# Both query tiles of two steps cast together and transposed together by DMA, a step ahead of their use

## The chip, the cores and the metric

The kernel runs on one core of one Trainium2 chip. In this kernel TensorE runs the matmuls; ScalarE, VectorE and GpSimd run the casts, copies and elementwise work; SyncE issues the DMA transfers. A transfer has landed when all of its data have arrived. The span is the time from the first to the last instruction of one profiled execution, and the granted clock is TensorE's clock as a share of full speed. The metric is the device time of one execution in microseconds, lower is better. An execution counts as slow when it lies over 1.5% above the fastest of the same kernel. A ratio here is the mean time of one kernel's fast runs over the mean of the other's fast runs of the same rounds, so it is not quite the ratio of the medians that I quote.

## The reference

A recurrent retention layer (decay per head) feeds a multiplicative feed-forward layer without a nonlinearity. Cut to what matters:

```python
# q, k, v: (4 batches, 8 heads, 768 positions, 64), fp32
for t in range(S):
    state = gamma * state + outer(k[:, :, t], v[:, :, t])
    y[:, :, t] = (1 / sqrt(D)) * q[:, :, t] @ state
x = y.transpose(0, 2, 1, 3).reshape(3072, 512)
out = ((x @ w1) * (x @ w2)) @ w3 @ w_out        # (3072, 512), fp32
```

## The kernel before

The recurrence is cut into chunks of 128 positions, two batches at a time: 12 steps. Step m begins on TensorE with the state part of the step before (`inter(m - 1)`), then the scores of chunk m, then the output matmuls of the feed-forward of two steps ago, then the feed-forward of the step before, with intra (the outputs from within the chunk) and kv (the update of the state) between. The scores need the queries and keys with the head dimension on the partitions, so q and k are cast to fp16 and then transposed by a DMA.

One query tile holds one batch and two chunks. So tiles 6 and 7 are read by steps 6 and 7, tiles 8 and 9 by steps 8 and 9, and the first half of the scores of a step (16 matmuls) reads the even tile, the second half the odd one.

```python
def load_q(n):                      # 512 KB, SyncE queue
    g, e = divmod(n, 2)
    ...
    dma_in(t[...], q[bp * 2 + e, :, cp * 2 * C : (cp + 1) * 2 * C, :]...)

def q_cast(n, eng):                 # fp32 -> fp16, two buffers
    q16 = att.tile([128, 1024], HP, tag="q16", name="q16", bufs=2)
    (nc.scalar.copy if eng is nc.scalar else eng.tensor_copy)(q16[...], q_in.pop(n)[...])

def q_dma(n):                       # transpose, five buffers, SyncE queue
    qT = att.tile([128, 2, NP, 128], HP, tag="qT", name="qT", bufs=5)
    nc.sync.dma_start_transpose(qT[...], q16s.pop(n)[:, :])

def queries(m, e, p, s, r):
    ...
    return qTs[m // 2 * 2 + e][half(r), :, p, i0 : i0 + 32]
```

Every load, every DMA transpose and every output of the kernel is issued by SyncE, in the order of the program. This is the step, which sets that order:

```python
def step(m):
    inter(m - 1); outputs_back(m - 1, 0); outputs_back(m - 1, 1)
    ...
    am_back = scores(m)
    am_back(0); am_back(1)
    if m > 5:
        q_dma(m + 2)
    ffn[m - 2].o_unit(0)            # 8 output matmuls, copy on ScalarE, output DMA
    if m + 1 < NSTEP:
        k_cast(m + 1, (nc.scalar,))
        k_dma(m + 1)                # transpose of k for the next step
    ffn[m - 2].o_unit(1)
    load_k(m + 2)
    load_v(m + 2)
    load_q(m + 3 if m < 6 else m + 4)
    for f in range(2):
        ffn[m - 1].ab(f)
    if m == 5:
        q_cast(7, nc.scalar)
        q_dma(7)
        load_q(9)
    intra(m)
    ...                             # kv, more ab
    v_cast(m + 1, (nc.gpsimd, nc.gpsimd))
    if m == 4:
        q_cast(6, nc.gpsimd)
        q_dma(6)
    elif m > 4:
        q_cast(m + 3, nc.gpsimd)
    ...
```

## Time and profile before

| | before |
|---|---|
| median of three runs | 198.76 us (197.88 to 199.11) |
| span of the profiled run | 196.1 us |
| TensorE busy | 92% |
| granted clock, mean | 0.983 |
| scores of step 4 start at | 73.70 us |
| step 6, from its scores to those of step 7 | 19.85 us |
| steps 4, 5, 7, 8, 9, 10, likewise | 12.16 to 12.24 us |

The prediction below shows the page, the stretches and the chain of waits. Two more views belong beside them. First the timeline of SyncE around step 5; columns: start, length, engine and line, operation, target and source, count. L60 is a load, L313 the transpose of q, L335 that of k, L490 an output. A line in which several are merged includes the waits between them.

```profile
87.57 2.48 SPq L313 DMA_TRANSPOSE qT<-q  x1
...
92.82 1.23 SPq L60 DMA_DIRECT2D stg<-in_k_dram  x2
94.09 3.05 SPq L60 DMA_DIRECT2D stg<-in_v_dram  x2
97.19 1.02 SPq L60 DMA_DIRECT2D stg<-in_q_dram  x1
98.31 2.36 SPq L313 DMA_TRANSPOSE qT<-q  x1
```

The first line is tile 6, the last tile 7. What to look for is the time SyncE spends on issuing: the two v loads alone take 3.05 us of its time. The timeline of TensorE has the other end of it; in brackets the idle time before the line and what ended it:

```profile
98.13 0.29 PE L358 MATMUL psA<-qT,kT 64*64 64x64 f16 x12
103.59 0.43 PE L358 MATMUL psA<-qT,kT 64*64 64x64 f16 x16 [5.16 <-DMA qT<-q]
```

The first half of the scores of step 6, on tile 6, runs at 98.13, and the second half waits 5.16 us for tile 7.

### The profile page before, as it was taken

How to read it: one execution, taken by the hardware profiler on the slowest of the kernel's cores; microseconds unless marked ns; L12 is line 12 of the kernel's file. 1: busy time of each engine (PE TensorE's matmuls, PEld its weight loads, DVE VectorE, ACT ScalarE, POOL GpSimd, SP SyncE). 2: the span in 40 equal slices, each digit the busy share in tenths (PEclk: the TensorE clock that was granted, in tenths of full speed). 3: DMA queues.
4: the chain of work that ended last, by engine and by line, in shares of the span. 5: the costliest groups of instructions: out<-in, count | busy, mean ns of one | idle time of the engine just before them, and what ended most of it. 6: DMA issues, size and time to landing. Idle time of an engine off the chain costs nothing.

```text
span 196.1 us, 6231 instructions
## 1 busy us (share of the span) xinstructions
PE 180.8 (92%) x2651; PEld 126.8 (65%) x2651; DVE 96.7 (49%) x187; ACT 87.5 (45%) x165; POOL 64.1 (33%) x92
## 2 busy tenths in 40 slices
PE   7799998679998999999908999999999999999993
PEld 2355655558675785877803685877858678586772
DVE  1226356068378255674432265664556735555240
ACT  5578545475553544327400544325443264232432
POOL 6200233536618071280601044280732607120000
PEclk9999999999999999999995899999999999999999
DMA  6999999999999999999998696989969550110202
GB/s 213 370 390 384 255 278 344 270 357 250 231 220 238 253 205 234 226 244 215 258 229 154 166 233 162 243 206 187 207 162 215 116 160 3 57 53 3 107 0 107
DMA packets 87338, 40.23 MB, mean 205 GB/s; under 512 B 67728, under 2 KB 82320, under 8 KB 87312
## 3 DMA queue, kind: packets, MB, share of 16 engines
q1 hardware_dynamic: 87312, 39.85, 84.0%
q8 instruction: 20, 0.33, 0.7%
q14 instruction: 6, 0.05, 0.1%
HBM read 29.36 MB, written 6.29 MB: 182 GB/s over the span
## 4 chain that ended last, share of the span: by engine, by line
PE 68%; SPq 12%; DMA 11%; DVE 4%; ACT 1%; issue 1%; DVEq 0%; ACTq 0%
PE psF L460 33%; PE psO L485 23%; SPq L60 12%; DMA stg<-in_moe_w_out_dram 4%; DMA stg<-in_k_dram 4%; DMA qT<-q 3%; PE psY L431 3%; PE psA L358 2%; PE psG L460 2%; PE psY L380 2%; PE psF L570 1%; DVE ht L475 1%; PE psK L400 1%; DVE am L365 1%; PE psTk L330 1%
## 5 line engine op out<-in xcount | busy, mean ns | idle before, releaser
L460 PE MATMUL psF<-xt,w 128*128 128x256 f16 x672 | 77.1, 273 | 0.0
L460 PEld LDWEIGHTS <-w 128*128 128x128 f16 x704 | 68.0, 98 | 10.3
L475 DVE TENSOR_TENSOR ht<-pa,psF 128x256 f16<-128x256 f32 x88 | 36.6, 420 | 54.3 <-ACT pa L469 29.7
L418 POOL TENSOR_TENSOR t<-s,GS 128x512 f16<-128x512 f32 x19 | 24.1, 1267 | 71.8 <-DVE s L417 71.8
L469 ACT COPY pa<-psF 128x256 f32<-128x256 f32 x80 | 29.7, 371 | 39.9 <-PE psF L460 39.9
L485 PE MATMUL psO<-w3o,ht 128*128 128x512 f16 (+2 forms) x200 | 46.2, 386 | 0.0
L485 PEld LDWEIGHTS <-ht 128*128 128x128 f16 x200 | 19.2, 101 | 21.5 <-issue 3.3
L489 ACT ACTIVATE osb<-psO 128x512 f32<-128x512 f32 (+2 forms) x25 | 14.5, 580 | 40.0 <-PE psO L485 40.0
L290 POOL TENSOR_TENSOR v<-stg,VS 128x512 f16<-128x512 f32 x23 | 23.5, 1042 | 5.5 <-DMA stg<-in_v_dram 3.9
L365 DVE TENSOR_TENSOR am<-psA,keep 128x512 f16<-128x512 f32 x24 | 15.3, 679 | 7.0 <-PE psA L358 7.0
L440 DVE TENSOR_TENSOR xt<-psY,YS 128x512 f16<-128x512 f32 x24 | 16.1, 722 | 1.7 <-PE psY L431 0.8
L269 POOL CAST q<-stg 128x1024 f16<-128x1024 f32 x8 | 8.3, 1036 | 23.6 <-DMA stg<-in_q_dram 23.6
L417 DVE TENSOR_TENSOR s<-psK,t 128x512 f32<-128x512 f32 x20 | 13.8, 688 | 3.4 <-PE psK L400 2.7
L283 ACT CAST k<-stg 128x1024 f16<-128x1024 f32 (+1 forms) x12 | 11.2, 934 | 5.1 <-DMA stg<-in_k_dram 4.9
L358 PE MATMUL psA<-qT,kT 64*64 64x64 f16 x384 | 6.6, 197 | 6.6 <-DMA qT<-q 5.2
L215 DVE COPY w3t<-psW 128x1024 f16<-128x1024 f16 x8 | 5.4, 689 | 11.7 <-PE psW L223 9.2
L358 PEld LDWEIGHTS <-kT 64*64 64x64 f16 x384 | 5.1, 108 | 8.1 <-issue 5.9
L196 ACT CAST w3h<-stg 128x1024 f16<-128x1024 f32 x8 | 8.3, 1043 | 3.6 <-DMA stg<-in_moe_w_dram 3.5
L431 PEld LDWEIGHTS <-t 64*64 64x64 f16 x352 | 6.5, 109 | 3.6 <-issue 2.1
L503 PE MATMUL psZ<-zeros 128*128 128x512 f16 x19 | 7.6, 553 | 1.3 <-DVE zeros L142 1.3
L431 PE MATMUL psY<-qT,t 64*64 64x64 f16 x352 | 7.8, 194 | 0.7 <-DVE t L418 0.6
L244 PE MATMUL psW<-wo,w3t 128*128 128x512 f16 x32 | 8.4, 399 | 0.0
(58 smaller groups left out, 121.2 us busy)
## 6 DMA issues: line engine op xcount, KB each, us to landing
stg<-in_moe_w_dram SPq DMA_DIRECT2D x16, 512.0 KB, 6.6
stg<-in_q_dram SPq DMA_DIRECT2D x12, 512.0 KB, 6.9
stg<-in_k_dram SPq DMA_DIRECT2D x24, 256.0 KB, 5.4
stg<-in_v_dram SPq DMA_DIRECT2D x24, 256.0 KB, 5.2
out_dram<-osb SPq DMA_DIRECT2D x23, 256.0 KB, 2.5
stg<-in_moe_w_out_dram SPq DMA_DIRECT2D x4, 512.0 KB, 7.8
out_dram<-osb SPq DMA_DIRECT2D x1, 160.0 KB, 1.8
qT<-q SPq DMA_TRANSPOSE x8, 4.0
```

Of the source, the lines that this page charges most:

```text
L60: nc.sync.dma_start(dst, src)
L290: eng.tensor_tensor(v16[:, e, :].rearrange("j (h d) -> j h d", d=D), v32[:, e, :].rearrange("j (h d) -> j h d", d=D), VS[:, :].unsqueeze(2 ...
L358: nc.tensor.matmul(ps[r][half(s), p * 2 + e, :], lhsT=kT[half(r), e, p, half(s)], rhs=queries(m, e, p, s, r), start=True, stop=True,)
L365: nc.vector.tensor_tensor(am[:, r, :, :], ps[r][:, :, :], keep[:, :].unsqueeze(1).broadcast_to((128, NP * 2, L)), MULT,)
L418: eng.tensor_tensor(t16[:, :], s32[:, :], gs, MULT)
L431: nc.tensor.matmul(ps[s][half(r), u, :], lhsT=t[s][half(r), u * L : (u + 1) * L], rhs=queries(m, e, p, s, r), start=False, stop=(e == 1 an ...
L440: nc.vector.tensor_tensor(XT[m][:, :, s, :].rearrange("p u (i t) -> p u t i", t=2), psYs[m][s][:, :, :].rearrange(order, t=2), YS[:, :, :] ...
L460: nc.tensor.matmul(ps[:, :], lhsT=W[d][:, f * 128 : (f + 1) * 128], rhs=self.x(d), start=(d == 0), stop=(d == 3),)
L469: nc.scalar.copy(self.pa[f][:, :], ps[:, :])
L475: nc.vector.tensor_tensor(self.HT[:, f, :], self.pa.pop(f)[:, :], ps[:, :], MULT)
L485: nc.tensor.matmul(psO[:, :], lhsT=self.HT[:, f, e * 128 : (e + 1) * 128], rhs=W3O[f][:, cs], start=(f == 0), stop=(f == 7),)
L489: nc.scalar.activation(osb[:, cs], psO[:, :], AF.Copy, scale=final_scale)
```

## The change

The intent is to have both tiles of a pair cast at the end of the even step and transposed at the front of the queue of the odd step, a whole step before the first matmul reads them. The special cases of steps 4 and 5 go. In even steps the query load moves ahead of the loads of k and v, so that it is there for the cast at the end of the same step. The whole diff:

```diff
--- before.py
+++ after.py
@@ -651,22 +651,20 @@
         am_back = scores(m)
         am_back(0)
         am_back(1)
-        if m > 5:
+        if m > 3 and m % 2:
+            q_dma(m + 1)
             q_dma(m + 2)
         ffn[m - 2].o_unit(0)
         if m + 1 < NSTEP:
             k_cast(m + 1, (nc.scalar,))
             k_dma(m + 1)
         ffn[m - 2].o_unit(1)
+        load_q(m + 3) if m % 2 == 0 else None
         load_k(m + 2)
         load_v(m + 2)
-        load_q(m + 3 if m < 6 else m + 4)
+        load_q(m + 3) if m % 2 else None
         for f in range(2):
             ffn[m - 1].ab(f)
-        if m == 5:
-            q_cast(7, nc.scalar)
-            q_dma(7)
-            load_q(9)
         intra(m)
         kv_back = kv(m)
         kv_back(0)
@@ -675,10 +673,8 @@
         kv_back(1)
         if m + 1 < NSTEP:
             v_cast(m + 1, (nc.gpsimd, nc.gpsimd))
-        if m == 4:
-            q_cast(6, nc.gpsimd)
-            q_dma(6)
-        elif m > 4:
+        if m % 2 == 0:
+            q_cast(m + 2, nc.gpsimd)
             q_cast(m + 3, nc.gpsimd)
         for f in range(4, 8):
             ffn[m - 1].ab(f)
```

## The prediction

> **What bounds the kernel now.** I read the page from the top: shares of the engines, then the span in 40 slices of 4.9 us (196.1 / 40), in tenths.
>
> ```profile
> span 196.1 us, 6231 instructions
> ...
> PE 180.8 (92%) x2651; PEld 126.8 (65%) x2651; DVE 96.7 (49%) x187; ACT 87.5 (45%) x165; POOL 64.1 (33%) x92
> ...
> PE   7799998679998999999908999999999999999993
> ...
> PEclk9999999999999999999995899999999999999999
> ```
>
> TensorE is busy for 92%; no other engine reaches 50%. From slice 10 on it stands at 8 or 9 (the last slice aside), except in slice 21 (98.0 to 102.9 us), where the digit is 0; right behind that hole the clock row dips to 5 and 8. So the kernel is bound by TensorE with one hole in it. I then cut the span where each step starts (at the inter matmuls of the step before). Stretches view, steps 4 to 8; columns: length, busy time of PE, PEld, DVE, ACT, POOL with counts, granted clock, DMA share, GB/s.
>
> ```profile
> 73.33:85.51 12.18, 12.18 (x213) 9.11 (x214) 7.08 (x14) 5.06 (x11) 4.53 (x5) 1.00 1.23 234
> 85.51:97.61 12.10, 12.10 (x194) 9.03 (x193) 6.57 (x13) 5.90 (x12) 5.30 (x6) 1.00 1.22 233
> 97.61:117.78 20.17, 15.01 (x213) 9.98 (x214) 7.18 (x14) 5.04 (x12) 3.25 (x3) 0.83 0.96 197
> 117.78:129.69 11.91, 11.91 (x196) 8.85 (x198) 6.99 (x14) 4.99 (x11) 5.52 (x6) 1.00 0.83 194
> 129.69:141.93 12.24, 12.24 (x213) 9.17 (x214) 6.99 (x14) 4.99 (x11) 5.51 (x6) 1.00 0.96 211
> ```
>
> Four steps last 11.9 to 12.2 us with TensorE always busy; step 6 lasts 20.17, with 5.16 us of it idle and a granted clock of 0.83. The mean of its four neighbours is 12.11, so step 6 costs 8.06 us too much. The chain of waits around it (start, length, what) says on what it stood:
>
> ```profile
> 94.09 2.04 SPq L60
> 96.13 0.04 issue
> 96.18 0.96 SPq L60
> 97.14 0.04 issue
> 97.19 1.02 SPq L60
> 98.21 0.05 issue
> 98.26 0.02 SPq L313
> 98.28 0.03 issue
> 98.31 5.24 DMA qT<-q
> 103.54 0.04 issue
> 103.59 0.43 PE psA L358 x12
> 104.02 6.03 PE psO L485 x16
> ```
>
> The scores of step 6 (L358) wait for a transposed query tile. Steps 6 and 7 read tiles 6 and 7; tile 6 was transposed at 87.57, so this is tile 7. SyncE issues its transpose only at 98.31, when the scores already want it, and it lands 5.24 us later. Yet its cast on ScalarE was finished at 93.15 (92.11 + 1.04, from the timeline of ScalarE). Between lie, in SyncE's order, one output, two k loads, two v loads and the load of tile 8: 92.16 to 98.21. Those 5.2 us in the queue are about the whole wait. Behind it, the 16 output matmuls take 6.03 us instead of the 3.56 us that the same 16 take in every step from 3 to 10.
>
> **What the Trainium skill says.** "TensorE: Matmul & The Clock Gate", Part 1, says that after an idle window of about 3.4 us the array falls to half clock and comes back after about as long a busy one. The trace agrees: 5.16 us idle, then 16 matmuls at 6.03 instead of 3.56, and a clock of 0.58 from 103.6 to 110.0. "DMA: Bandwidth & Descriptors", Anatomy of one DMA, says that the DMA engines do not wait on semaphores; the wait sits on the issuing sequencer. So what stands behind a waiting or slow issue in SyncE's program waits too: the 92.16 to 98.31 above. The same page, Rules for kernel authors, says to issue early and wait late, which is this change's intent. "GPSIMD Engine Reference", 4.1 Engine selection, calls one-input work there roughly line-rate; here the cast of a query tile takes 1036 ns on GpSimd and 1045 ns on ScalarE, so moving it costs nothing in itself.
>
> **The change part by part.** Steps 0 to 3 issue the same things in the same order, so up to about 81 us nothing moves. No matmul is added or removed.
>
> *Loads.* In even steps the query load goes ahead of k and v. Tile 7's load moves from 85.19 to about 81.1, where the k load stood. It landed 6.9 us after issue before (85.19 to the cast at 92.11), so now it lands at about 88. The k and v loads of that step go back by its issue of about 1.1 us; k lands some 5 us after issue, at about 88, and its cast started at 88.77: just in time. Tile 9's load leaves step 5, which so has one 512 KB load less.
>
> *Casts.* Both on GpSimd at the end of the even step, after the v casts (which ended at 86.5): tile 6 at 86.5 to 87.55 as before, tile 7 at 87.6 or 88 (when it has landed) to 89.1 at the latest. ScalarE loses 1.04 us in step 5. GpSimd then has nothing to do until 93.2 (the next state update, L418), so two casts fit; neither engine is on the path.
>
> *Transposes.* They become the first things in SyncE's queue in step 5: tile 6 at 87.57 as before, since it waited for the same cast, and tile 7 right after, between 89.1 and 90.1. An issue took 1.24 to 2.48 us and a landing 3.0 to 5.4 us. Tile 7 therefore lands at about 94 to 95.5, against 103.5 before and a need at 98.1. The wait is gone with 2.5 us to spare.
>
> *What goes behind.* The output and the transpose of k for step 6 were issued at 90.15 and 90.78; a further transpose ahead of them (1.24 to 2.48) puts k's at about 92 to 93.3, and with 3.8 to 5.7 us to landing (the extremes of steps 4 and 5) at 95.8 to 99. It is needed at 98.1. This is the one place with little room. The loads behind it have a whole step in hand.
>
> *Buffers.* Five transposed tiles are kept; tile 9 takes the place of tile 4, last read at the start of step 6, and it is transposed in step 7; tile 7's place was tile 2's, done with in step 4. Two cast tiles are kept and both are read before the next pair is cast. No new wait.
>
> *The sum.* Idle before the scores 5.16, plus half clock on the output matmuls 6.03 - 3.56 = 2.47: 7.63 us. By steps it is 8.06 (the scores and first blocks after the hole were slow too). I take 7.8. All of it is on the path, since TensorE is full on either side and nothing waits in its place. 198.76 - 7.8 = 191.0. Against it stands k's transpose in step 6: a chance of about 1 in 4 of a wait of about 1 us, 0.3 us on average. Prediction 191.3 us.
>
> **The rivals.** *A wait on k's transpose takes the place of the one on q.* For it: three transposes behind one another when the DMA share is 1.22. In step 2 to 3 the trace has just that: two query transposes at 64.84 and 66.5 and k's at 68.73, which landed 4.1 us later, with no wait on it. Against it: step 5 has a load less. If it happens, 0.3 to 1.5 us idle, too short for the clock to fall: 191.5 to 192.5. If it passed 3.4 us, the clock would fall too and most of the gain would be lost: 195 to 198; I give that 3%.
>
> *The DMA queues become the bound.* Without the hole the transfers no longer have 8 us to catch up. A step moves k, v, q and the output, 0.524 MB each, and two transposes of 0.262: 2.6 MB in 12.1 us, 217 GB/s. Steps 4 and 5 moved 234 and 233 GB/s with TensorE full. Odd steps now have three transposes, 2.9 MB or 238 GB/s, even ones 2.4 MB. So it fits on average, and loads are used one step or more later. A wait of up to 2 us in steps 7 or 9 would give 191.5 to 193.5; 10%.
>
> *The casts come late:* tile 9 is loaded in step 6 and cast at its end. The load stands 7.7 us into the step (81.1 - 73.4) and lands some 7 us later, 14.7 into it; the cast is wanted 14 us in. Its transpose then starts in step 7 perhaps 1 us late, in front of the outputs and k's transpose, which had over 4 us in hand in steps 7 and 8 (121.82 plus 3.1 against scores at 130.3). It is hidden.
>
> *The hole was a matter of one run:* the three timings of before lie within 197.88 to 199.11, so the hole of 7.8 us was in all.
>
> **Range and chances.** The best is 198.76 - 8.06 with the spread of the runs (0.9 below the median): 189.9. The worst that I give weight is a new wait of 2 to 3 us: 194. Within 2% means above 194.8, so over 3 us of new waits; with the two rivals that could do it I get 0.06, and 0.01 for slower by 2%.
>
> **What would show it.** Right: TensorE's row has no 0 and the clock no 5 after slice 10; step 6 lasts about 12.2 us; no wait of a matmul on a transposed query; ScalarE has three query casts in place of four and GpSimd nine; both transposes of a pair stand together ahead of the outputs in steps 5, 7 and 9. Wrong: a wait of L358 on the transpose of k in step 6 (first rival), waits on v or k casts in steps 7 to 9 (second), or a transpose of tile 9 that starts late in step 7 and takes the outputs with it (third).

## The result and the profile after

The changed kernel took 192.64 us (median of four runs: 192.71, 195.71, 192.57, 192.49; the second was a slow one), against 198.94 for the kernel before in the same rounds: ratio of the fast runs 0.9698, 95% interval 0.9648 to 0.9749. In three later batches it was 0.9571, 0.9629 and 0.9604, each with its own profile.

The page of the kernel after, parts 1 and 2:

```profile
span 191.0 us, 6232 instructions
...
PE   7799998768998969999999999999999999999993
...
PEclk9999999999999999999999999999999999999999
```

There is no 0 in the row of TensorE after the start and no dip in the clock. After slice 10 one lesser digit stands in slice 15 (a 6); it is explained below. The stretches view of the kernel after, cut 0.2 us after the scores of steps 6 and 7 begin (columns as in the prediction):

```profile
100.77:112.70 11.93, 11.93 (x216) 8.83 (x207) 6.85 (x14) 5.00 (x11) 2.50 (x3) 1.00 1.23 245
112.70:125.22 12.52, 12.32 (x231) 9.07 (x220) 6.85 (x15) 4.91 (x11) 6.77 (x7) 1.00 1.16 200
```

Step 6 now takes 11.93 us with TensorE busy in all of it; step 7 has 0.20 us of idle. The timeline of SyncE in steps 4 and 5 shows why:

```profile
83.43 0.42 SPq L60 DMA_DIRECT2D stg<-in_q_dram  x1
83.94 2.53 SPq L60 DMA_DIRECT2D stg<-in_k_dram  x2
86.57 2.55 SPq L60 DMA_DIRECT2D stg<-in_v_dram  x2
90.10 4.20 SPq L313 DMA_TRANSPOSE qT<-q  x2
94.39 0.54 SPq L490 DMA_DIRECT2D out_dram<-osb  x1
95.04 2.59 SPq L335 DMA_TRANSPOSE kT<-k  x1
```

Both transposes of q stand ahead of the outputs. The second was issued at 93.05 and landed 3.2 us later, at 96.25; the scores of step 6 began at 100.58. The transpose of k behind them landed 4.5 us after its issue, at 99.54: 1.0 us before the scores.

Where the time went, step by step, from the start of one step's scores to those of the next (us; the column at the right is the second profile of the changed kernel, from the first batch of experiments):

| stretch | before | after | after, second profile |
|---|---|---|---|
| start to scores of step 4 | 73.70 | 76.23 | 74.03 |
| step 4 | 12.18 | 12.18 | 12.18 |
| step 5 | 12.16 | 12.16 | 12.16 |
| step 6 | 19.85 | 11.93 | 11.93 |
| step 7 | 12.17 | 12.53 | 12.23 |
| steps 8 to 10 | 36.61 | 36.55 | 36.55 |
| scores of step 11 to end | 29.42 | 29.42 | 29.42 |
| span | 196.09 | 191.00 | 188.51 |

The change gave 7.92 us in step 6 in both profiles. In the first, 2.53 us of it are missing because the part before step 4 was longer, and 0.36 in step 7. Of the 2.53, 1.49 us are one wait in step 3; this is the timeline of TensorE there:

```profile
69.24 0.60 PE L460 MATMUL psF<-xt,w 128*128 128x256 f16 x4 [1.49 <-ACT osb L489]
```

On ScalarE an output copy stood behind the cast of k tile 4, which waited for its load. The same happened in small in step 7, where the timeline of ScalarE reads:

```profile
116.49 1.05 ACT L283 CAST k<-stg 128x1024 f16<-128x1024 f32 x1 [1.01 <-DMA stg<-in_k_dram]
117.44 0.59 ACT L489 ACTIVATE osb<-psO 128x512 f32<-128x512 f32 x1
```

The k load of an even step now stands behind the query load, and the cast of that k tile, one step later, waits; the output copy behind it frees a bank of PSUM (the memory that matmuls write to) late, and TensorE stops for 0.2 us. That the place of the k load is the reason is read from the traces and was not tested alone: in the four profiles of the changed kernel the k casts of steps 6, 8 and 10, whose loads stand ahead of a query load, never wait, and those of step 7 wait 0.52 to 1.01 us. The place is not the only reason: the k cast of step 4, whose load also stands ahead of a query load, waits 0.30 to 0.89 us.

### The profile page after: what moved, and what is told of

Its sections match the earlier page's. It is cut to its first block, busy times and chain, and to the rows that moved or that the text cites. A ratio compares the mean times of both kernels' runs of the same rounds, so it can differ in the third digit from the quotient of the medians.

```text
span 191.0 us, 6232 instructions
## 1 busy us (share of the span) xinstructions
PE 178.9 (94%) x2651; PEld 125.4 (66%) x2651; DVE 96.8 (51%) x187; ACT 86.0 (45%) x164; POOL 65.1 (34%) x93
## 4 chain that ended last, share of the span: by engine, by line
PE 65%; DMA 18%; SPq 10%; ACT 3%; issue 1%; DVE 0%; ACTq 0%
PE psF L460 37%; PE psO L485 20%; SPq L60 10%; DMA stg<-in_moe_w_dram 7%; DMA stg<-in_k_dram 7%; DMA stg<-in_moe_w_out_dram 5%; PE psY L431 3%; PE psY L380 2%; PE psA L358 2%; PE psK L400 1%; ACT w L196 1%; ACT k L283 1%; ACT osb L489 1%; PE psTk L330 0%; ACT kT L196 0%
## 5 line engine op out<-in xcount | busy, mean ns | idle before, releaser
L460 PE MATMUL psF<-xt,w 128*128 128x256 f16 x672 | 77.4, 273 | 1.7 <-ACT osb L489 1.7
L485 PE MATMUL psO<-w3o,ht 128*128 128x512 f16 (+2 forms) x200 | 43.7, 371 | 0.0
L485 PEld LDWEIGHTS <-ht 128*128 128x128 f16 x200 | 18.5, 98 | 19.6
L269 POOL CAST q<-stg 128x1024 f16<-128x1024 f32 x9 | 9.2, 1039 | 17.8 <-DMA stg<-in_q_dram 17.8
L570 PE MATMUL psF<-xt,w 128*128 128x256 f16 x64 | 8.0, 273 | 0.9 <-POOL w L590 0.4
L244 PE MATMUL psW<-wo,w3t 128*128 128x512 f16 x32 | 8.6, 408 | 0.0
L257 PE MATMUL psW<-wo,w3t 128*128 128x512 f16 x32 | 8.1, 380 | 0.0
```

The source lines that it names most:

```text
L460: nc.tensor.matmul(ps[:, :], lhsT=W[d][:, f * 128 : (f + 1) * 128], rhs=self.x(d), start=(d == 0), stop=(d == 3),)
L485: nc.tensor.matmul(psO[:, :], lhsT=self.HT[:, f, e * 128 : (e + 1) * 128], rhs=W3O[f][:, cs], start=(f == 0), stop=(f == 7),)
```

## The experiments

Theory: tile 7 was late because its transpose stood in SyncE's queue behind the loads of step 5; the hole cost an idle part and a clock part. Rivals: its late load and cast were the cause; or the hole, or the start, was chance. All twelve runs gave correct results.

| run | median, us | ratio to before | 95% interval | rounds |
|---|---|---|---|---|
| before_again | 199.25 | 0.9976 | 0.9919 to 1.0032 | 3 |
| after_again | 191.12 | 0.9571 | 0.9511 to 0.9632 | 3 |
| late_transpose | 200.56 | 0.9941 | 0.9836 to 1.0047 | 3 |
| order_only | 195.56 | 0.977 | 0.97 to 0.9841 | 3 |
| fill_hole | 197.42 | 0.9878 | 0.9838 to 0.9917 | 5 |
| order_two | 192.84 | 0.9641 | 0.9587 to 0.9695 | 5 |
| k_on_pool | 191.5 | 0.9585 | 0.9546 to 0.9625 | 5 |
| after_third | 192.74 | 0.9629 | 0.9584 to 0.9675 | 5 |
| fill_again | 197.08 | 0.985 | 0.981 to 0.9889 | 3 |
| q_behind | 196.53 | 0.9826 | 0.9776 to 0.9876 | 5 |
| k_pool_two | 191.28 | 0.9565 | 0.9526 to 0.9604 | 5 |
| after_fourth | 192.27 | 0.9604 | 0.9573 to 0.9636 | 5 |

The first four rows are one batch, the next four another, the last four a third.

### The two kernels again: before_again, after_again, after_third, after_fourth

No edit.

> The kernel before, unchanged, for a second profile. If the hole in step 6 is built into the order of the issues (theory), it is there again: 4.5 to 6 us of idle before the scores of step 6 on the transpose of query tile 7, and a clock below 1 behind it. Rival: it was a chance of one profile, then it is gone or elsewhere. The start (to the scores of step 3) shall say how far it varies: 61.7 us in the first profile; if the changed kernel's 62.5 and its 1.5 us stall in step 3 are chance, this one may show such things too.

The hole was there: 6.12 us of idle before the second half of the scores of step 6, on the transpose of q, a little over the range expected. The start to the scores of step 4 took 73.76 us. So the hole belongs to the order of the program; its size varies by about a microsecond.

> The changed kernel, unchanged, for a second profile: ratio 0.97 to the kernel before. Theory: the 1.5 us idle in step 3 (a matmul that waits for an output copy behind the cast of k tile 4) is a matter of when the early loads land, since nothing before step 4 was changed; it may be gone (then 190.5 to 191.5 us) or be there again (192.5). Steps 4 to 11 take 97.5 us in both cases. Rival: the stall comes from the change; then it is always in the changed kernel and never in the one before.

> The changed kernel, unchanged, beside the others of this call as their measure. Ratio 0.957 to 0.97; a stall in step 3 behind the cast of k tile 4 in some profiles and not in others.

> The changed kernel, unchanged, as the measure for this call: ratio 0.957 to 0.97.

The three further profiles of the changed kernel have no hole in step 6 (11.93 us in each). The stall in step 3 was in none of them. The start to the scores of step 4 took 74.03, 76.05 and 74.89 us. Its parts differ: in after_third the clock stood at half for 6.83 us from about 39 to 46 us; after_fourth lost 0.72 us in step 5 to an output copy behind the cast of k tile 6, which waited 1.53 us for its load. So the stall of step 3 is not in every execution of the changed kernel. Nor is it foreign to the order of the kernel before: order_only and order_two, which leave everything before step 5 as it was, have the same stall, 0.29 and 0.54 us on an output copy behind the cast of k tile 4. The rival, that the stall comes from the change, has fallen. Whether the start as a whole is longer in it is not settled. Five profiles whose program up to step 4 and whose step 4 are those of the kernel before (before, before_again, order_only, order_two, fill_again) have 73.70 to 75.54 us, 74.3 on average; the other eight, with the changed step 4 (fill_hole left out), have 74.03 to 76.23, 75.3 on average. No instruction that is issued before step 4 has another place in the order, except that k_on_pool and k_pool_two move a k cast in step 3. Four of the eight (after_third, after_fourth, q_behind, k_on_pool) fell back to half clock once within the start and none of the five did; beyond that I know no cause and claim none.

### Put the cause back alone: late_transpose

```diff
 # in the changed kernel
         if m > 3 and m % 2:
             q_dma(m + 1)
-            q_dma(m + 2)
+            if m != 5:
+                q_dma(m + 2)
 ...
         for f in range(2):
             ffn[m - 1].ab(f)
+        if m == 5:
+            q_dma(7)
```

> The changed kernel with one line put back: in step 5 the transpose of query tile 7 stands behind the loads of k, v and q again; its load and its cast stay early. Theory (place in the issuing queue is the cause): the hole before the scores of step 6 is back, 3.5 to 6 us with the clock down behind it, time 197 to 200 us, 3 to 4% over the changed kernel. Rival (what made tile 7 late was its late load and late cast): no hole, 192 to 193 us.

The time went back to that of the kernel before. Two of its four runs count as slow, the profiled one among them (201.0 us; the fast ones were 197.53 and 200.12), so I use the profile for the order of things only. GpSimd had both casts early, by its timeline:

```profile
88.35 2.02 POOL L269 CAST q<-stg 128x1024 f16<-128x1024 f32 x2
```

and yet the chain of waits of the same run (start, length, what) goes through the load in front of the transpose:

```profile
99.09 1.11 SPq L60
...
100.30 5.66 DMA qT<-q
105.96 0.04 issue
106.00 0.43 PE psA L358 x13
```

Tile 7 was cast by 90.37 and its transpose issued at 100.30. A load and a cast that are early do not help a transpose that stands late in the queue. The rival of the late load and cast has fallen.

### Cure it by order alone: order_only and order_two

```diff
 # in the kernel before, step 5 only
-        load_k(m + 2)
-        load_v(m + 2)
-        load_q(m + 3 if m < 6 else m + 4)
+        if m != 5:
+            load_k(m + 2); load_v(m + 2); load_q(m + 3 if m < 6 else m + 4)
         for f in range(2):
             ffn[m - 1].ab(f)
         if m == 5:
             q_cast(7, nc.scalar)
             q_dma(7)
+            load_k(7); load_v(7); load_q(8)     # order_two: load_q(8) first
             load_q(9)
```

> The kernel before with one change: in step 5 the loads of k, v and q are issued behind the transpose of tile 7, not in front; load order, cast and casting engine of tile 7 stay as before. Theory: the transpose is issued at the end of its cast at about 93.2 us and not at 98.3, lands at about 97 to 98.5 (needed at 98.1), so 0 to 0.5 us of hole are left and no fall of the clock: 191 to 192.5 us, ratio 0.96 to 0.97. Rival (late load and cast): the hole stays, 198.8 us.

The hole of step 6 was gone, with tile 7 loaded and cast as in the kernel before (step 6 from 98.80). But only some 2.3% came of it, since a new wait had opened one step later. TensorE's timeline:

```profile
113.86 0.44 PE L358 MATMUL psA<-qT,kT 64*64 64x64 f16 x32 [2.88 <-DMA kT<-k]
```

Tile 8's load, now the last but one of the late loads, landed late, so GpSimd cast it at 106.57 after 9.34 us of waiting; its transpose, first in the queue of step 6, was issued at 107.64 and not earlier; and the transpose of k for step 7 stood behind it, at 109.61. The clock is worth a look too, in the stretches view of order_only:

```profile
110.98:114.80 3.82, 0.94 (x36) 0.64 (x36) 1.86 (x4) 0.00 (x0) 1.67 (x2) 1.00 0.90 247
115.00:118.20 3.20, 3.20 (x9) 1.07 (x8) 0.64 (x2) 0.96 (x2) 0.00 (x0) 0.50 1.31 234
```

After an idle stretch of 2.88 us the clock fell, and it did so about a microsecond after TensorE had work again (113.86): the 16 output matmuls took 5.25 us and not 3.56. The last section says what decides this.

> As order_only, but the load of q tile 8 is issued right behind the transpose of tile 7, in front of k and v. Theory: what spoilt order_only was that tile 8's load came 6 us late, its cast too, and its transpose then held back the outputs and the transpose of k behind it in the issuing queue; with the load early there is no wait on k in step 7 over 0.5 us: 191 to 192.5 us on the chip of the first case, ratio 0.957 to 0.965, as the changed kernel. Rival (one transpose per step is itself worse than a pair): 2.9 us of wait in step 7 stay, ratio 0.977.

With the load of tile 8 in front, no matmul waited on a transpose in step 7 and the ratio was 0.9641, beside 0.9629 for the changed kernel in the same batch. So the place in the queue, of tile 7's transpose and of tile 8's load, is all that the gain needs. The pairing, the casts on GpSimd and the whole step of lead are one way of having it; a further gain from them is not to be seen within the intervals (about 0.5% to either side).

### Keep TensorE busy in the hole: fill_hole and fill_again

```diff
 # in the kernel before
+        if m == 6:
+            fill = ps_f.tile([128, 512], FP, tag="psF", name="psZ")
+            for _ in range(22):
+                nc.tensor.matmul(fill[:, :], lhsT=Z[:, 0:128], rhs=Z[:, 0:512], start=True, stop=True)
         am_back = scores(m)
```

> The kernel before with 22 matmuls on a tile of zeros put in front of the scores of step 6 (22 x 0.222 us = 4.9 us), so that TensorE works while it waits for tile 7. Nothing else moves; the transpose lands when it did. Theory (the cost is an idle part and a clock part): the scores still end at the landing of tile 7, but the clock stays at 1.00 and the 16 output matmuls behind take 3.56 us and not 6.03: 2.5 us faster, ratio 0.987. Rival (all of the cost is the wait, or the slow outputs are slow for another reason): outputs at 6.0 us, ratio 1.00.

> fill_hole again, because its profile fell on an execution in which TensorE ran at half clock from end to end (366.7 us), while its five other runs took 197.2 to 197.9 us. Theory: in an ordinary execution no half clock after the start, the 16 output matmuls behind the filler in 3.56 us, 197.5 us, ratio 0.988. Rival: the profile shows the outputs at 6 us and the gain from elsewhere.

The ratios were 0.9878 and 0.985: 2.4 and 3.0 us of 200. The profile of fill_hole fell on an execution of 368.38 us in which TensorE ran at about half speed throughout (the filler took 10.27 us; why is not known); its other five runs took 197.2 to 197.92. The profile of fill_again is an ordinary one; TensorE's timeline:

```profile
98.57 4.92 PE L654 MATMUL psZ<-zeros 128*128 128x512 f16 x22
...
105.12 0.32 PE L358 MATMUL psA<-qT,kT 64*64 64x64 f16 x16 [1.38 <-DMA qT<-q]
105.37 3.63 PE L485 MATMUL psO<-w3o,ht 128*128 128x512 f16 x16
```

Tile 7 came no sooner, but the outputs behind it ran at full clock (3.63 us in the timeline, which counts the last matmul's tail; the same view has 6.10 for the kernel before). So of the roughly 7.9 us of the hole some 2.5 to 3 are the clock and the other 5 the wait.

### Undo one part: q_behind

```diff
 # in the changed kernel
-        load_q(m + 3) if m % 2 == 0 else None
         load_k(m + 2)
         load_v(m + 2)
-        load_q(m + 3) if m % 2 else None
+        load_q(m + 3)
```

> The changed kernel with one part undone: in even steps the query load stands behind k and v again, as before. Theory: tile 7 then lands some 4 us later, at about 94.5, is cast at 95.5 on GpSimd, and its transpose, first in the queue of step 5, holds back the outputs and the transpose of k for step 6, which lands at 101 to 103 and is wanted at 100.7: new waits on the transpose of k of 0.5 to 2.5 us in steps 6, 8 and 10, in all 1 to 6 us, ratio 0.965 to 0.99. Rival: hidden, because the pair is cast a whole step ahead; ratio as the changed kernel, 0.957 to 0.963.

It cost over half of the gain: 0.9826 beside 0.9604. GpSimd's timeline in step 5 has the late load, and SyncE's has what it held back (the line spans both transposes and the wait between them):

```profile
93.43 1.04 POOL L269 CAST q<-stg 128x1024 f16<-128x1024 f32 x1 [4.34 <-DMA stg<-in_q_dram]
```

```profile
89.12 7.11 SPq L313 DMA_TRANSPOSE qT<-q  x2
96.32 0.53 SPq L490 DMA_DIRECT2D out_dram<-osb  x1
96.95 1.30 SPq L335 DMA_TRANSPOSE kT<-k  x1
```

SyncE was held for 7.11 us where the changed kernel needs 4.20. Scores waited on the transpose of k for 0.24, 0.69 and 0.68 us in steps 6, 8 and 10, less than I expected; two matmul groups of steps 8 and 10 waited 0.77 and 1.38 us on output copies, which stood on ScalarE behind casts of k that had waited 1.58 and 2.19 us for their loads. So the head of the queue is a good place only for what is ready: a transpose that waits there for its cast delays everything behind it. Moving the query load ahead of k and v is a needed part of the change.

### The cast of k on GpSimd too: k_on_pool and k_pool_two

```diff
 # in the changed kernel, step(m)
-            k_cast(m + 1, (nc.scalar,))
+            k_cast(m + 1, (nc.gpsimd,))
```

> The changed kernel with the cast of the next step's k tile on GpSimd and not on ScalarE (steps 3 to 10). Where a k load lands late the cast then no longer stands in front of an output copy on ScalarE, so the stall of 1.5 us in step 3 and of 0.2 us in step 7 that the first profile of the changed kernel showed cannot occur. Expected 0 to 1.5 us under the changed kernel (0.5 on average), ratio 0.953 against 0.957. Rival: GpSimd, with two query casts before it in odd steps, makes k's transpose late: waits of scores on the transpose of k, slower by 1 us or more.

> k_on_pool again, beside the changed kernel on the same chip. If its gain is real, 0.3 to 0.6% under the changed kernel again and no wait of a matmul on an output copy; if not, equal within 0.2%.

The two profiles have no wait of a matmul on an output copy and none on the transpose of k. The medians were 191.5 beside 192.74, and 191.28 beside 192.27. Against the kernel before the ratios are 0.9585 beside 0.9629 and 0.9565 beside 0.9604. That is 0.4% twice in the same direction; the 95% intervals of each pair overlap, so it is likely and not beyond doubt. From the scores of step 4 to those of step 11 it took 84.99 and 84.93 us, against 85.35, 85.06, 85.15 and 86.09 in the four profiles of the changed kernel: a gain of 0.07 to 1.16 us where it was meant to be. Within a batch the two profiles differ there by 0.16 and 1.16 us, while the medians differ by 1.24 and 0.99, so not all of the difference is shown to be the gain intended.

## Why the prediction was right

The 192.64 us lie inside the range of 189.9 to 194.0, 1.3 us above the point. (The sum behind the lower end, 198.76 - 8.06 - 0.88, gives 189.8.) As a ratio the prediction is 0.9625; measured were 0.9698 and, in the later batches, 0.9571, 0.9629 and 0.9604.

- **The bound and the hole.** "An idle part and a clock part, all of it on the path": step 6 fell by 7.92 us, where the prediction had 7.63 from the chain, 8.06 from the steps, and took 7.8. Filling the hole shows the clock part apart, 2.4 to 3.0 us by the ratios, where it had 2.47.
- **The cause.** That tile 7 was late by its place in the queue is shown from both sides: late_transpose brings the hole back with tile 7 cast 10 us ahead; order_two takes it away with tile 7's load and cast as they were.
- **The landing of tile 7.** Predicted 94 to 95.5 with the need at 98.1; it landed at 96.25 with the scores at 100.58, in a trace that runs 2.5 us later there. The distance to the scores was 4.3 us where the prediction had 2.6 to 4.1.
- **The one tight place.** The transpose of k was predicted to land between 2.3 us ahead of the scores and 0.9 us behind; it landed 1.0 us ahead, and no scores waited for it. The first rival did not come about in the form that was told. A smaller kin did: the k loads, put back behind the query load, made the casts of k late on ScalarE, and an output copy behind them cost 0.2 us in step 7, and 0.72 in step 5 of another profile. The prediction had called that load "just in time" and had given it no cost of its own; from the scores of step 4 to those of step 11, the four profiles of the changed kernel lie 0.07 to 1.10 us, 0.42 on average, above the version without that wait (k_on_pool, 84.99). That this is near the 0.3 us that were allowed for another reason is luck.
- **The other rivals.** DMA did not become the bound: from the scores of step 6 on, no matmul of the changed kernel's first profile waited on a transfer directly. But the sign that the prediction names for this rival, a wait of a k cast in steps 7 to 9, did appear (1.01 us in step 7, 0.42 in step 9); of it only 0.20 us reached TensorE. Tile 9's cast was not late: the two casts at the end of step 6 ran back to back.
- **What it did not see.** The part before step 4 was 2.5 us longer in the first profile than in that of before, and in that execution it, not the change's own steps, is why 192.7 and not about 190 was measured. The other runs of that round have no profile. In the second batch the median was 191.12. The prediction took this part as fixed. Two profiles of before would have said how steady it is, but only one was at hand.
- **A wrong step in a rival.** "Too short for the clock to fall", said of waits of up to 1.5 us with a limit at 3.4 us, holds for the 1.38 and 1.49 us waits seen in fill_again and after. But the length of one wait is not what decides: 2.88 us in order_only and 1.65 us in the start of after_third were followed by half clock (last section). A wait on k's transpose in the changed kernel could have cost more than the prediction gave it; none arose.

## What to carry to other kernels

Where one engine issues all transfers, its program order is a schedule: look in the timeline for when a transfer became ready and when it was issued, for the gap between the two is queueing and can be cured by order alone. Put at the head of a step what is ready and needed soonest, and never what has yet to wait, since everything behind it waits too. And look whether a hole in TensorE costs more than its length: here a 5 us wait cost 7.9 us, because the clock fell and the work behind it ran at half speed.

## What the Trainium skill lacked or had wrong

- "TensorE: Matmul & The Clock Gate", Part 1 (table of the two states, and "HAM oscillation"): its rule of thumb sets the limit for idle gaps at about 3.4 us. In these profiles that is too generous, and the length of one gap does not decide. In order_only a gap of 2.88 us led to 3.41 us of half clock, which began about 1 us after TensorE had work again; in after_third a gap of 1.65 us led to 6.83 us of it (38.97 to 45.80), and in k_pool_two a gap of 1.65 us to none; in k_on_pool and q_behind 3.41 us of it began at 41.67 and 41.89 though no gap in the 4 us before was over 0.72 us. What does fit is the free-running window that the same page describes: in every profile that records the clock, its changes lie whole multiples of 3.413 us apart. I cut the spans, after the first 6 us, into these windows. At full clock, each of the 10 windows with TensorE busy for under 1.7 us was followed by half clock, 2 of the 9 with 1.7 to 2.06 us were, and none with more. So a short gap costs clock or not by how it falls on the windows; this is worked out from these traces alone, and the ends of matmuls in them are modelled.
- "TensorE: Matmul & The Clock Gate", Part 1, also says that the clock has been seen stuck low for 50 us and more. One execution of fill_hole agrees: it took 366.7 us at about half speed, while the clock that its profile states was 1.00. The times of the matmuls show it (10.27 us for a filler of 4.92), the stated clock does not.
- "DMA: Bandwidth & Descriptors", "Issuing engines are not separate DMA queues": it calls the issuing time "usually small relative to the DMA itself". In the profiles of before and after one transpose held SyncE for 1.24 to 2.84 us with 3.0 to 5.7 us to landing, and the pair of v loads of step 5 in the kernel before held it for 3.05 us. Such issues, one behind another, held tile 7's transpose back for 5.2 us.
